# Pairing a convolution kernel's spectra by adding transfers in DRAM

## The chip, the cores and the metric

The kernel runs on one core of a Trainium2 chip. The metric is the device time of one execution in microseconds (us). The core has a matrix engine (PE), a vector engine (VectorE, DVE in the profile), an activation engine (ScalarE, ACT), GpSimd (POOL) and SyncE (SP). Each works through its own queue of instructions in order, and they wait for each other on semaphores. DMA transfers are issued by SP and GpSimd; in this kernel only GpSimd's transfers add to what lies at the destination.

## The reference

The program is two layers of the same pair: a long convolution over time (an S4 state-space layer) and a gated feed-forward net, each on a normalised input and with a residual. L = 2048 time steps, D = 512 channels, N = 128 states, F = 1376.

```python
dt = exp(log_dt);  A = A_re + 1j*A_im;  dB = dt * (B_re + 1j*B_im)
K = einsum("dn,dnl,dn->dl", C, exp((dt*A)[:, :, None] * l), dB).real   # one kernel of 2048 lags per channel
conv(u) = irfft(rfft(u, 2L) * rfft(K, 2L))[:L] + u * Dskip             # causal convolution and the direct term
x = x + conv(layernorm(x))
x = x + (silu(n @ w_gate) * (n @ w_up)) @ w_down                       # n = layernorm(x)
# ... and both lines once more with the same weights
```

The direct term `u * Dskip` is the same as adding `Dskip` to the kernel at lag 0. K depends on the parameters alone and is computed once, for both layers.

## The kernel before, in words

The program has two parts. The first, called the kernel stage here, computes K and its spectra and stores them in DRAM (array `wdr`) and in SBUF (`w0r`, for the first time block). The second runs the convolutions and the feed-forward nets block by block (512 time steps each) with products of spectra; it reads `wdr` from about 299 us on.

The kernel stage goes through the channels in eight chunks of 64 (DC, NCH). For one chunk:

- `gen_turns`, `gen_exp`, `gen_trig` (VectorE, ScalarE) make powers of the states; `gen_g` and `gen_e` (VectorE) make from them the two factors `g` and `re`/`im` of every lag. The last doubling step of `gen_g` is added by a GpSimd transfer from `acc` into `g` (L465).
- `lags` (PE, L485 and L486) multiplies the factors into `pk`: all 2048 lags of 64 channels.
- `spread_in` copies `pk` to `ks` (ScalarE, L491), and `spread` turns it round through DRAM (`kdr`) into `kt` (SP, L498 and L500); the last two chunks do it on PE instead (`spread_pe`).
- `spectra`, called for q0 = 0 and q0 = 1, multiplies `kt` with Fourier matrices on PE (`products`, L515) into the PSUM tile `pw`: two of four frequency classes q at a time, real and imaginary part i, NB = 4 blocks k of 512 lags. L517 adds the direct term as a product of a row of ones with `dsk`. What the convolution needs for block k is the sum of block k and of a signed, swapped copy of block k-1. ScalarE writes the signed copy of blocks 0 to 2 into `wo` (L542, twice) and block 0 into `w0r` (L543), VectorE adds blocks 1 to 3 from PSUM (L545), and SP stores the sum (`store_w`, L524): two transfers of 192 KB, in rows of 256 B.

Chunks 6 and 7 do part of this later by `first_parts` and `later_parts`, among the first convolution.

Beside the chunks run the sums of squares of the weights (`norms`): GpSimd loads a piece `st` (L317; three buffers under the tag w, which `scales` and the convolution use later), ScalarE squares it (L323), PE adds it over partitions into `nrm` (L326), and at the end of a group VectorE takes the maximum (L329). `second` computes input spectra `pf` (L289, L292, L293).

The order of all this is written out by hand. `at(t, f)` puts a step on a list with a time on a scale of about microseconds; `starts` holds each chunk's start, 28 or 31 apart; the list is sorted and run, and within `manual_schedule` the engines that it names issue in just this order. Before the change these are ScalarE, VectorE and PE, and SP in the chunk loop; GpSimd's order is found by the planner from its own estimates. `spectra` is a generator with four parts (products; ScalarE's copies; VectorE's addition; SP's stores), and `use` gives the time of each part. After the stage the planner orders every engine.

The tags name buffers: a tile waits until the last user of the tile before it under the same tag is done. `z` has one buffer, free in this stage; `sg` has one (for `wo` with q0 = 0), and with q0 = 1 `wo` is a piece of `spare`.

Of the kernel before, what the change touches and what calls it, by code (L numbers as in the profile page):

```python
# [11 lines left out]
F32 = mybir.dt.float32  # L12
# [10 lines left out]
P = 128  # L23
# [11 lines left out]
DC = 64  # L35
# [38 lines left out]
def kernel(ctx, tc, x, a_re, a_im, b_re, b_im, c_re, c_im, log_dt, d_skip,  # L74
# [62 lines left out]
    G.memset(ones, 1.0)  # L137
    onesb = sb.tile([P, P], BF16, name="onesb")
    G.memset(onesb, 1.0)
    one = sb.tile([P, 1], F32, name="one")  # L140
    G.memset(one, 1.0)
    hpi = sb.tile([P, 1], F32, name="hpi")
    G.memset(hpi, math.pi / 2)

# [333 lines left out]
    def lags(ts, g):  # L478
# [7 lines left out]
            PE.matmul(o, lhsT=g[:, 1, :, d], rhs=im[:, 0:64, d], start=False, stop=True, tile_position=(0, 32 * grp))  # L486
        return pk

    def spread_in(pk):
        ks = tl([P, 4, 16, 16], "ks", "nn")  # L490
        A.activation(ks, pk.rearrange("p d (c a) -> p a c d", a=4), AF.Copy)  # L491
        return ks
# [15 lines left out]
                          start=True, stop=True, tile_position=(0, 32 * ga))  # L508
        A.activation(kt, kp, AF.Copy)

    def products(ch, pw, kt, k0, k1, q, order):

        for i, c in order:
            e = ek[q // 2][:, q % 2, c - 1, i] if c else ef[:, q, i]
            PE.matmul(pw[:, i], lhsT=e, rhs=kt[:, :, c + 4 * k0:4 * k1:4, :].rearrange("p g k d -> p k g d"), start=c == 0, stop=c == 3)  # L515
            if (i, c) == (0, 0) and k0 == 0:
                PE.matmul(pw[:, 0, 0], lhsT=one[0:1].to_broadcast([1, P]), rhs=dsk[:, ch * DC:(ch + 1) * DC], start=False, stop=False)  # L517

    def signs(q):

        return enumerate((-1.0, 1.0) if q % 2 == 0 else (1.0, -1.0))

    def store_w(h, off, q, wo):
        nc.sync.dma_start(wdr[1:, h, q, :, :, off:off + DC].rearrange("k p i d -> p i k d"), wo.rearrange("p i k g d -> p i k (g d)"))  # L524

    def spectra(ch, kt, q0):


        h, off = ch // 4, (ch % 4) * DC
        pw = pbig([P, 2, 2, NB, 4, 16], "pw")  # L530
        for j in range(2):
            products(ch, pw[:, j], kt, 0, NB, q0 + 2 * j, [(i, c) for i in range(2) for c in range(4)])
        yield
        if q0:
            wo = spare[0][:, 16 * DC:].rearrange("p (j i k g d) -> p j i k g d", j=2, i=2, k=NB - 1, g=4)
        else:
            wo = tl([P, 2, 2, NB - 1, 4, 16], "wo", "sg")
        wf = pw.rearrange("p j i k g d -> p j i k (g d)")
        wv = wo.rearrange("p j i k g d -> p j i (k g d)")
        pv = pw.rearrange("p j i k g d -> p j i (k g d)")  # L540
        for i, sign in signs(q0):
            A.activation(wv[:, :, i], pv[:, :, 1 - i, :3 * DC], AF.Copy, scale=sign)  # L542
        A.activation(w0r[:, h, q0::2, :, off:off + DC], wf[:, :, :, 0], AF.Copy)  # L543
        yield
        V.tensor_tensor(wv, pv[:, :, :, DC:], wv, OP.add)  # L545
        yield
        for j in range(2):
            store_w(h, off, q0 + 2 * j, wo[:, j])
        yield

    def first_parts(c0, q):

        n, off = NCH - c0, (c0 % 4) * DC
        pw = pbig([P, 2, 8, 4, 16], "pw")[:, :, :n]
        for c in range(4):
            for i in range(2):
                e = ek[q // 2][:, q % 2, c - 1, i] if c else ef[:, q, i]
                PE.matmul(pw[:, i], lhsT=e, rhs=kt2[:, c0 + 2 - NCH:, :, c], start=c == 0, stop=c == 3)
                if (i, c) == (0, 0):
                    PE.matmul(pw[:, 0], lhsT=one[0:1].to_broadcast([1, P]), rhs=dsk[:, c0 * DC:], start=False, stop=False)  # L560
        A.activation(w0r[:, 1, q, :, off:], pw.rearrange("p i k g d -> p i (k g d)"), AF.Copy)

    def later_parts(ch, kt, qs=QORD):


        h, off = ch // 4, (ch % 4) * DC
        for q in qs:
            pw = psml([P, 2, NB - 1, 4, 16], "pw")
            products(ch, pw, kt, 1, NB, q, [(0, c) for c in range(4)])
            yield  # L570
            products(ch, pw, kt, 1, NB, q, [(1, c) for c in range(4)])
            yield
            w0 = w0r[:, h, q, :, off:off + DC].rearrange("p i (g d) -> p i g d", g=4)
            wo = next(slots)
            for i, sign in signs(q):
                A.activation(wo[:, i, 0], w0[:, 1 - i], AF.Copy, scale=sign)
                A.activation(wo[:, i, 1:], pw[:, 1 - i, :2], AF.Copy, scale=sign)
            V.tensor_tensor(wo, pw, wo, OP.add)
            store_w(h, off, q, wo)
            yield  # L580
# [344 lines left out]
                if m:  # L925
                    tops.append(m)

    with tc.manual_schedule(engines={mybir.EngineType.Activation, mybir.EngineType.DVE, mybir.EngineType.PE}):
        ts[0], ts[1] = gen_tiles(0), gen_tiles(1)
        ex = gen_exp(0, ts[0])  # L930

# [54 lines left out]
        def at(t, f, n=1):  # L986
            plan.append((t, len(plan), (lambda: take(f, n)) if hasattr(f, "__next__") else f))
# [17 lines left out]
        def factors(c, t):  # L1005

            at(t + 0.2, lambda: upper(ts[c]))

            def tiles():
                gs[c] = tl([P, 2, 32, DC], "g", ("ga", "gb")[c % 2])  # L1010
            at(t + 0.1, tiles)
            gg, ge = later(lambda: gen_g(c, ts[c], gs[c])), later(lambda: gen_e(ts[c]))
            for k in range(4):
                at(t + 0.2 + 2 * k, gg, 2)
            at(t + 0.3, ge)
            for k in range(5):
                at(t + 8.2 + k, gg)
            at(t + 22.0, ge, 100)

        def use(c, t):  # L1020

            box, kt, n = {}, kt2[:, c % 2], starts[c + 1]

            def copy():
                box["ks"] = spread_in(box["pk"])
                if c < NCH - 2:
                    spread(c, box["ks"], kt)
            at(t, lambda: box.update(pk=lags(ts[c], gs[c])))
            at(t + 7.1, copy)
            if c == NCH - 2:  # L1030
                at(t + 10.0, lambda: spread_pe(box["ks"], kt))
            at(t + 25.0, lambda: sizes(c, kt, box["ks"]))
            for q0, ats in list(enumerate(((t + 17.5, t + 25.2, n + 2.1, n + 9.0),
                                      (n + 6.9, n + 14.0, n + 17.3, n + 22.0))))[:2 if c < NCH - 2 else 1]:
                sp = later(lambda q0=q0: spectra(c, kt, q0))
                for t0 in ats:
                    at(t0, sp)
# [26 lines left out]
        for i in range(NCH - 1):  # L1064
# [3 lines left out]
            second_block(i, t)  # L1068
            if i + 2 < NCH:
                prepare(i + 2, t)  # L1070
            for k, t0, t1, t2, t3 in ((0, -1.4, 8.0, 13.9, 17.0), (1, 8.1, 14.5, 17.45, 19.5),
                                      (2, 15.0, 26.5, 28.05, 36.0)):
                n = ((3, 3, 0), (3, 3, 0), (3, 3, 0), (3, 2, 0), (3, 2, 0), (3, 3, 0), (3, 3, 3))[i][k]
                if i == NCH - 2 and k == 2:
                    t0, t1, t2, t3 = 15.0, 20.0, 24.0, 27.0
                if n:
                    weights(n, t + t0, t + t1, t + t2, t + t3)
# [53 lines left out]
        norm = first_norm(tl([P, 2, D], "nn1", "hf"))  # L1131
        take(conv[0], 1)
        spread_pe(ks, kts[1])
        take(conv[0], 1)
        scales()
        split(1, 0)
# [99 lines left out]
```

## Time and profile before

| | us |
|---|---|
| median of three executions | 1191.86 |
| lowest and highest | 1186.78, 1192.82 |
| the profiled execution | 1186.51 |
| its span in the profile | 1184.7 |
| PE, VectorE, ScalarE, GpSimd busy | 1117.3, 1006.2, 587.1, 92.2 |
| lag products of chunk 0 and chunk 7 end (ks copy starts) | 69.18, 274.26 |

In the rows of the profile, L515 is a line of the kernel, then come the engine and the operation, written tile <- read tiles, sizes as partitions x elements, and a count. In a timeline the first two numbers are the start and the length in us of a run of equal instructions, and square brackets hold how long the engine had been idle before and what it waited for. An fp32 matmul appears as two rows. A row of POOL with DMA_DIRECT2D is the time in which GpSimd makes a transfer, not the transfer itself; in the list of DMA issues the last number is the median time from issue to landing. In the view by source line the three numbers behind the count are minimum, median and maximum in ns. In the stretch view each engine has its busy time and its number of instructions, then come the granted clock, the share of the DMA engines and GB/s.

### The profile page before, as it was taken

The page shows a single profiled execution, that of the slowest core. Times are in us where ns is not written, and L with a number is a line of the kernel's source. Part 1 is how long each engine was busy: PE and PEld are TensorE (multiplying, and loading weights), DVE is VectorE, ACT ScalarE, POOL GpSimd, SP SyncE. Part 2 cuts the span into 40 slices and gives each one's busy share as a digit, 9 for nine tenths or more (in the row PEclk, how much of TensorE's full clock was granted, in tenths as well). Part 3 has the DMA queues.
Part 4 walks back from the last instruction along what each step waited for, and adds up shares of the span by engine and source line. Part 5 has one row for each costly group of instructions (what it writes and reads, how often), then busy time and mean ns, then how long its engine had stood idle before and what let it go on. Part 6 is the DMA issues. An engine that isn't in the chain of part 4 may idle for free.

```text
span 1184.7 us, 24523 instructions
## 1 busy us (share of the span) xinstructions
PE 1117.3 (94%) x10008; PEld 884.8 (75%) x10008; DVE 1006.2 (85%) x1591; ACT 587.1 (50%) x1180; POOL 92.2 (8%) x151
## 2 busy tenths in 40 slices
PE   1979999999789988999999999989999999999998
PEld 1868888888776857777778687858777686876875
DVE  7999999987789898999899999989994899983211
ACT  6677888833461554546654443655533452324211
POOL 1011111110000010002000000211000010000000
PEclk9989999999899999999999999999999999999999
DMA  6266666757484337432353354333544144312000
GB/s 231 91 162 149 162 166 162 182 179 240 125 271 140 115 119 200 118 96 84 92 152 128 112 165 155 96 104 115 149 116 165 46 121 130 118 49 45 14 24 18
DMA packets 136532, 151.17 MB, mean 128 GB/s; under 512 B 75474, under 2 KB 83666, under 8 KB 136419
## 3 DMA queue, kind: packets, MB, share of 16 engines
q1 hardware_dynamic: 129314, 126.47, 35.8%
q0 software_dynamic: 7104, 23.14, 7.3%
q8 instruction: 78, 1.28, 0.5%
q14 instruction: 36, 0.29, 0.1%
HBM read 101.85 MB, written 31.46 MB: 113 GB/s over the span
## 4 chain that ended last, share of the span: by engine, by line
PE 37%; DVE 27%; issue 4%; DMA 4%; ACT 2%; SPq 1%; POOL 0%; DVEq 0%; ACTq 0%; POOLq 0%
PE pgu L886 6%; PE pgu L887 6%; PE pgu L889 6%; DVE t L754 5%; DVE yk L757 5%; PE py L901 4%; PE py L902 3%; PE py L903 3%; PE pi L773 3%; PE pf L273 3%; DVE yk L754 2%; DVE z L229 2%; DVE sg L893 2%; DMA mix<-nn 1%; DVE bb L229 1%
## 5 line engine op out<-in xcount | busy, mean ns | idle before, releaser
L886 PE MATMUL pgu<-mix,wsl 128*128 128x256 f16 x1280 | 299.7, 273 | 6.9 <-DVE sg L893 4.4
L887 PE MATMUL pgu<-mix,wsl 128*128 128x256 f16 x1280 | 299.7, 273 | 0.0
L889 PE MATMUL pgu<-mix,wsl 128*128 128x256 f16 x1280 | 195.6, 273 | 0.0
L887 PEld LDWEIGHTS <-wsl 128*128 128x128 f16 x1280 | 125.5, 98 | 24.3 <-issue 8.0
L901 PE MATMUL py<-wsl,hh 128*128 128x512 f16 (+1 forms) x352 | 134.2, 381 | 8.6 <-DVE xg L906 6.9
L886 PEld LDWEIGHTS <-wsl 128*128 128x128 f16 x1280 | 125.4, 98 | 16.0
L889 PEld LDWEIGHTS <-wsl 128*128 128x128 f16 x1280 | 125.5, 98 | 14.9
L903 PE MATMUL py<-wsl,hl 128*128 128x512 f16 (+1 forms) x352 | 134.1, 381 | 0.2 <-DVE hl L895 0.2
L902 PE MATMUL py<-wsl,hh 128*128 128x512 f16 x320 | 121.8, 381 | 0.0
L754 DVE TENSOR_TENSOR t<-uu,w 128x1024 f32<-128x1024 f32 x96 | 116.9, 1218 | 2.6 <-DMA w<-wdr 2.4
L757 DVE TENSOR_TENSOR yk<-yk,t 128x1024 f32<-128x1024 f32 x96 | 116.9, 1217 | 0.3
L892 ACT ACTIVATE sg<-pgu,sc 128x512 f32<-128x512 f32 x80 | 54.6, 683 | 121.0 <-PE pgu L889 115.9
L893 DVE SCALAR_TENSOR_TENSOR sg<-pgu,sc,sg 128x512 f32<-128x512 f32 x80 | 59.6, 745 | 56.6 <-ACT sg L892 56.5
L515 PE MATMUL pw<-kt,ek 128*128 128x256 f32 (+1 forms) x384 | 94.1, 382 | 0.0
L894 ACT ACTIVATE hh<-sg 128x512 f16<-128x512 f32 x80 | 50.0, 626 | 76.1 <-DVE sg L893 76.0
L773 PE MATMUL pi<-yl,mix 128*128 128x256 f16 x576 | 78.9, 273 | 5.0 <-DVE yl L229 2.7
L515 PEld LDWEIGHTS pw<-kt,ek 128*128 128x128 f32 x384 | 70.8, 194 | 8.9
L273 PE MATMUL pf<-z,eh 128*128 128x256 f16 x576 | 74.9, 273 | 0.0
L754 DVE TENSOR_TENSOR yk<-u,w0r 128x1024 f32<-128x1024 f32 x56 | 68.2, 1218 | 1.5 <-ACT u L275 1.5
L902 PEld LDWEIGHTS <-hh 128*128 128x128 f16 (+1 forms) x352 | 34.6, 98 | 46.1 <-issue 10.6
L895 DVE TENSOR_TENSOR hl<-sg,hh 128x512 f16<-128x512 f32 x80 | 54.8, 686 | 15.6 <-ACT hh L894 15.5
L485 PE MATMUL pk<-re,g 128*32 128x64 f32 x1024 | 65.0, 317 | 2.8 <-DVE re L440 2.8
(239 smaller groups left out, 2154.3 us busy)
## 6 DMA issues: line engine op xcount, KB each, us to landing
w<-wdr SPq DMA_DIRECT2D x96, 256.0 KB, 2.7
uu<-udr SPq DMA_DIRECT2D x96, 256.0 KB, 3.0
udr<-u POOLq DMA_DIRECT2D x32, 256.0 KB, 2.7
g<-acc POOLq DMA_DIRECT2D x6, 1024.0 KB, 8.4
udr<-u SPq DMA_DIRECT2D x16, 256.0 KB, 2.1
n<-ndr SPq DMA_DIRECT2D x16, 256.0 KB, 3.9
n<-xdr SPq DMA_DIRECT2D x4, 1024.0 KB, 5.7
kdr<-ks SPq DMA_DIRECT2D x6, 512.0 KB, 2.7
```

Source lines behind the costliest of these rows:

```text
L273: PE.matmul(pf[:, o], lhsT=e, rhs=m, start=k == 0, stop=k == len(terms) - 1)
L515: PE.matmul(pw[:, i], lhsT=e, rhs=kt[:, :, c + 4 * k0:4 * k1:4, :].rearrange("p g k d -> p k g d"), start=c == 0, stop=c == 3)
L754: V.tensor_tensor(t, uu.unsqueeze(1).to_broadcast([P, 2, 2, HD]), w.unsqueeze(2).to_broadcast([P, 2, 2, HD]), OP.mult)
L757: V.tensor_tensor(yk, yk, t, OP.add)
L773: PE.matmul(pi[:, o], lhsT=e, rhs=m, start=k == 0, stop=k == len(terms) - 1)
L886: PE.matmul(o, lhsT=wgu(wi, k, 0)[:, fs], rhs=nh[:, k], start=k == 0, stop=False)
L887: PE.matmul(o, lhsT=wgu(wi, k, 1)[:, fs], rhs=nh[:, k], start=False, stop=False)
L889: PE.matmul(o, lhsT=wgu(wi, k, 0)[:, fs], rhs=nlo[:, k], start=False, stop=k == 3)
L893: V.scalar_tensor_tensor(sg, pgu[:, 1], sc6[:, 4:5], sg, OP.mult, OP.mult)
L901: PE.matmul(py[:, r], lhsT=hh[:n, f, rc], rhs=wd(f, 0)[:n], start=f == 0, stop=False)
L902: PE.matmul(py[:, r], lhsT=hh[:n, f, rc], rhs=wd(f, 1)[:n], start=False, stop=False)
L903: PE.matmul(py[:, r], lhsT=hl[:n, f, rc], rhs=wd(f, 0)[:n], start=False, stop=f == FT - 1)
```

## The change

Three things change, all in the kernel stage.

1. The direct term leaves the products: L517 and L560 (the same in `first_parts`) go, and a new step `skip` adds `dsk` to lag 0 of `kt` on VectorE, on the first partition.
2. The sum of the two copies is made in DRAM. ScalarE copies blocks 1 to 3 from PSUM into a new tile `wa` (tag z), SP stores the signed copy `wo`, and GpSimd then issues the same two transfers from `wa` with an addition. VectorE's L545 goes. The parts of `spectra` are now products; ScalarE's copies; SP's stores; GpSimd's adding transfers.
3. GpSimd is named in `manual_schedule`, so its instructions go out in source order. Some times change with it: the last part of `spectra`, the maxima of the weights' sums, and the four last steps of `gen_e`, which are now separate entries.

```diff
+    def skip(ch, kt):
+
+        k = kt[0:1, :, 0]
+        V.tensor_tensor(k, k, dsk[:, ch * DC:(ch + 1) * DC].rearrange("p (g d) -> p g d", g=4), OP.add)
...
-    def products(ch, pw, kt, k0, k1, q, order):
+    def products(pw, kt, k0, k1, q, order):
...
-            if (i, c) == (0, 0) and k0 == 0:
-                PE.matmul(pw[:, 0, 0], lhsT=one[0:1].to_broadcast([1, P]), rhs=dsk[:, ch * DC:(ch + 1) * DC], start=False, stop=False)
...
-    def store_w(h, off, q, wo):
-        nc.sync.dma_start(wdr[1:, h, q, :, :, off:off + DC].rearrange("k p i d -> p i k d"), wo.rearrange("p i k g d -> p i k (g d)"))
+    def store_w(h, off, q, wo, eng=nc.sync, **add):
+        eng.dma_start(wdr[1:, h, q, :, :, off:off + DC].rearrange("k p i d -> p i k d"), wo.rearrange("p i k g d -> p i k (g d)"), **add)
...
+        wa = tl([P, 2, 2, NB - 1, 4, 16], "wa", "z")
...
             A.activation(wv[:, :, i], pv[:, :, 1 - i, :3 * DC], AF.Copy, scale=sign)
+        A.activation(wa.rearrange("p j i k g d -> p j i (k g d)"), pv[:, :, :, DC:], AF.Copy)
         A.activation(w0r[:, h, q0::2, :, off:off + DC], wf[:, :, :, 0], AF.Copy)
-        yield
-        V.tensor_tensor(wv, pv[:, :, :, DC:], wv, OP.add)
         yield
         for j in range(2):
             store_w(h, off, q0 + 2 * j, wo[:, j])
+        yield
+        for j in range(2):
+            store_w(h, off, q0 + 2 * j, wa[:, j], G, accum_op=OP.add)
         yield
...
-                if (i, c) == (0, 0):
-                    PE.matmul(pw[:, 0], lhsT=one[0:1].to_broadcast([1, P]), rhs=dsk[:, c0 * DC:], start=False, stop=False)
...
-    with tc.manual_schedule(engines={mybir.EngineType.Activation, mybir.EngineType.DVE, mybir.EngineType.PE}):
+    with tc.manual_schedule(engines={mybir.EngineType.Activation, mybir.EngineType.DVE, mybir.EngineType.PE, mybir.EngineType.Pool}):
...
-            at(t + 22.0, ge, 100)
+            for k in range(4):
+                at(t + 22.0 + 0.6 * k, ge, 1 if k < 3 else 100)
...
+            at(t + (17.1 if c < NCH - 2 else 12.5), lambda: skip(c, kt))
...
-            for q0, ats in list(enumerate(((t + 17.5, t + 25.2, n + 2.1, n + 9.0),
-                                      (n + 6.9, n + 14.0, n + 17.3, n + 22.0))))[:2 if c < NCH - 2 else 1]:
+            for q0, ats in list(enumerate(((t + 17.5, t + 25.2, n + 2.1, n + 7.5),
+                                      (n + 6.9, n + 14.0, n + 17.3, n + 21.0))))[:2 if c < NCH - 2 else 1]:
...
-            for k, t0, t1, t2, t3 in ((0, -1.4, 8.0, 13.9, 17.0), (1, 8.1, 14.5, 17.45, 19.5),
+            for k, t0, t1, t2, t3 in ((0, -1.4, 8.0, 13.9, 22.3), (1, 8.1, 14.5, 17.45, 22.9),
...
         spread_pe(ks, kts[1])
+        skip(c, kts[1])
```

In `weights(n, t0, t1, t2, t3)` the four times are those of a group's loads, squares, products and maximum.

More of the change, by code (lines that the diff above doesn't have):

```diff
@@ L531, in spectra @@
         for j in range(2):
-            products(ch, pw[:, j], kt, 0, NB, q0 + 2 * j, [(i, c) for i in range(2) for c in range(4)])
+            products(pw[:, j], kt, 0, NB, q0 + 2 * j, [(i, c) for i in range(2) for c in range(4)])
         yield
@@ L568, in later_parts @@
             pw = psml([P, 2, NB - 1, 4, 16], "pw")
[L569 removed]
+            products(pw, kt, 1, NB, q, [(0, c) for c in range(4)])
             yield
[L571 removed]
+            products(pw, kt, 1, NB, q, [(1, c) for c in range(4)])
             yield
```

2 lines of the change are left out of this document (removed).

## The prediction

> **What bounds the kernel now.** I read the page first, then the stretch view, then the timelines of PE, ScalarE, VectorE and GpSimd over one round of the kernel stage, and last the groups and DMA issues of what the change touches. The stage handles eight chunks of 64 channels, and a round runs from the end of one chunk's lag products (L485, L486) to the next.
>
> ```profile
> span 1184.7 us, 24523 instructions
> PE 1117.3 (94%) x10008; PEld 884.8 (75%) x10008; DVE 1006.2 (85%) x1591; ACT 587.1 (50%) x1180; POOL 92.2 (8%) x151
> ...
> 98.20:242.90 144.70, 144.70 (x1750) 122.91 (x1750) 139.00 (x164) 118.44 (x264) 22.76 (x43) 1.00 0.68 170
> ```
>
> In the 144.7 us of five rounds PE has no gap (columns PE, PEld, DVE, ACT, POOL), at full clock. VectorE is idle for only 5.7 us, ScalarE for 26.3. PE paces the stage and VectorE is close behind, so the page's 50% for ScalarE says nothing about this stage.
>
> ```profile
> 127.45 0.70 PE L515 MATMUL pw<-kt,ef 128*128 128x256 f32 x2
> ...
> 139.46 0.60 PE L326 MATMUL nrm<-sq,onesb 128*128 128x344 bf16 x3
> 139.90 0.59 PE L515 MATMUL pw<-kt,ef 128*128 128x256 f32 x2
> 140.43 0.43 PE L517 MATMUL pw<-tdk,one 1*128 1x64 f32 x2
> ...
> 142.18 0.59 PE L515 MATMUL pw<-kt,ef 128*128 128x256 f32 x2
> ...
> 143.91 0.59 PE L515 MATMUL pw<-kt,ef 128*128 128x256 f32 x2
> ...
> 148.01 0.49 PE L485 MATMUL pk<-re,g 128*32 128x64 f32 x8
> ...
> 156.37 0.70 PE L515 MATMUL pw<-kt,ef 128*128 128x256 f32 x2
> ```
>
> This round is 127.45 to 156.37 = 28.9 us; below, E is its start (127.45) and times are after E. PE does one spectrum (q0=1 of the chunk before), squares' sums (nrm) and pf, at E+12.0 the second nrm group, then spectrum q0=0, and at E+20.6 the lag products, 8.4 us.
>
> ```profile
> 127.64 1.02 ACT L491 ACTIVATE ks<-pk 128x1024 f32<-128x1024 f32 x1 [4.78 <-PE pk L486]
> 128.56 1.24 ACT L323 ACTIVATE sq<-st 128x344 bf16<-128x344 f32 x3
> ...
> 135.77 0.87 ACT L542 ACTIVATE spare<-pw 128x384 f32<-128x384 f32 x2
> 136.53 0.39 ACT L543 ACTIVATE w0r<-pw 128x256 f32<-128x256 f32 x1
> 136.79 1.26 ACT L323 ACTIVATE sq<-st 128x344 bf16<-128x344 f32 x3
> 138.07 1.28 ACT L395 ACT_TABLE_LOAD   x1
> ...
> 148.29 0.93 ACT L542 ACTIVATE wo<-pw 128x384 f32<-128x384 f32 x2
> ```
>
> ScalarE is idle once a round, 4.8 us before ks. It ends the second group of squares at 138.05, 1.4 us before PE needs it (139.46).
>
> **The change part by part.** *Direct term out of the products.* Eight products without it take 143.91-142.18 = 1.73 us, with it 142.18-139.90 = 2.28. Each of the two-pass L517 rows thus costs 0.55 us, 2.2 us in a round of four. PE alone would need 28.9-2.2 = 26.7.
>
> *Direct term into lag 0 (skip).* One VectorE addition of 64 elements on one partition. L454 (64 elements on 128 partitions, 0.22, row below) is nearest; I take 0.25 us. It waits for the kt loads, and behind it wait L435 and all later E-steps on VectorE, and PE's products. In the steady round it stands where the second L545 stood, at E+10.5, with the last kt load issued about 1.5 into the row below and landed 3.6 later, E+9.1, and PE there at E+11.5; in the first round VectorE comes later than PE:
>
> ```profile
> 78.71 2.74 DVE L386 CUSTOM_DVE_ANT_0 im<-im 128x256 uint16<-128x256 uint16 x4
> 81.37 2.29 DVE L435 TENSOR_TENSOR re<-re 128x2048 f32<-128x2048 f32 x1
> ...
> 79.42 0.67 PE L515 MATMUL pw<-kt,ef 128*128 128x256 f32 x2 [1.06 <-DMA kt<-kdr]
> ...
> 131.39 2.04 SPq L500 DMA_DIRECT2D kt<-kdr  x4
> ```
>
> There skip stands behind the doubling L386 until 81.4, so the products start 2.3 us later; less two L517 this round loses 1.2.
>
> *L545 off VectorE.*
>
> ```profile
> 121.95 0.95 DVE L545 TENSOR_TENSOR wo<-pw,wo 128x768 f32<-128x768 f32 x1
> 122.82 0.22 DVE L454 TENSOR_TENSOR g<-g,spare 128x64 f32<-128x64 f32 x1
> ...
> 138.86 0.95 DVE L545 TENSOR_TENSOR spare<-pw,spare 128x768 f32<-128x768 f32 x1
> 139.73 2.28 DVE L435 TENSOR_TENSOR re<-re 128x2048 f32<-128x2048 f32 x1
> ```
>
> By their starts 0.87 us each, 1.74 a round, less 0.25 for skip: VectorE's busy time falls from 139.0/5 = 27.8 to 26.3 a round, below PE's. The moved maxima (L329) and the split of the four E-steps change no amount of work; they put the maxima where their sums exist.
>
> *A third copy (wa) on ScalarE.* 768 elements out of PSUM lie between the 384 of L542 (0.87/2) and the 1024 of L491 (0.92 by starts): 0.75 us, 1.5 a round, inside the 4.8 idle. But the one at E+9.1 stands before the second squares, whose end moves from E+10.6 to E+11.35, while PE, two L517 shorter, now wants it at E+10.9. So PE waits 0.4; from there 0.15 for the last nrm, 8.1-1.1 for the spectrum and 8.4 for the lags make a round of 26.95. Every further us X that ScalarE stands still before those squares lengthens the round by X: the gain is 2.0-X, and the 1.4 us of cover at this place is what hid it before.
>
> *Where X comes from: the adding transfers.* wa has one buffer. Its copy at E+9.1 waits until both adding transfers of the spectrum before have landed. These run on GpSimd's queue, 384 KB in two, each of 768 pieces of 256 B.
>
> ```profile
> L465 POOL DMA_DIRECT2D g<-acc x6: 1237/1272/1294, 78.4 to 225.6; - x6
> L317 POOL DMA_DIRECT2D st<-in_B_w_gate_dram x16: 536/556/584, 101.3 to 187.0; - x16
> L706 POOL DMA_DIRECT2D udr<-u x32: 539/542/607, 410.9 to 886.4; - x32
> ...
> g<-acc POOLq DMA_DIRECT2D x6, 1024.0 KB, 8.4
> ...
> kt<-kdr SPq DMA_DIRECT2D x24, 128.0 KB, 3.6
> ...
> xg<-in_A_u_dram SPq DMA_DIRECT2D x3, 1024.0 KB, 5.7
> ...
> st<-in_B_w_gate_dram POOLq DMA_DIRECT2D x16, 172.0 KB, 3.4
> ...
> wdr<-wo SPq DMA_DIRECT2D x14, 192.0 KB, 3.4
> ```
>
> GpSimd's time G for one: L317 (172 KB) and L706 (256 KB) have 128 pieces and the same 0.54 to 0.56, so pieces count and not bytes; the only adding one, L465, has 256 and 1.27, that is 5.0 ns a piece. For 768 that is 3.8 us. The ends are 0.55 (a price per transfer) and 0.54+640*5.7 ns = 4.2 (the slope from 128 to 256). I take 3.8, from the row that also adds. R, from the end of G to landing: 3.4-0.6 = 2.8 as the plain store of the same pieces from SP, up to 8.4-1.3 = 7.1 as L465; the 1 MB addition lands 1.5 times as late as a 1 MB load (8.4 against 5.7), so I take 3.5.
>
> [...]
>
> The clock of the chain: the signed copies of q0=0 (148.29, E+20.8) move 0.75 later with the wa before them and end at E+22.5, 4.5 before the next E. SP stores at once (these stores moved ahead of kdr and kt in SP's queue, which is empty there), the first lands 3.4 later, and GpSimd starts at E-1.0. Landed: E-1.0+2G+R = E+10.1, wanted E+9.1, so X = 1.0. Behind the wait stand w0r, the second squares, and through PE's nrm the spectrum and the lags. Behind the pair on GpSimd stand, in source order now, the three loads for the second squares (0.55 each; the last is issued at E+7.7 and lands 3.4 later at E+11.1, wanted at E+10.95+X: covered), then the memsets and L465, which lands at E+8.3+8.4 = E+16.7, 1.8 before the lags need it. The other adding pair starts at E+12.6 and lands at E+23.7; wa wants its buffer at E+22.6, and the 1.1 fits into what is left of ScalarE's idle time. The loads for the next round's first squares follow at E+20.2 and land at E+24.7, 3 before they are wanted. GpSimd's round is 4*3.8 + 6*0.55 + 1.3 = 20 of 28 us. The new bytes could also hold up the kt loads (3.6); PE has 1 us of slack there, I add nothing and leave it to the range.
>
> **Sum.**
>
> ```profile
> 69.18 1.02 ACT L491 ACTIVATE ks<-pk 128x1024 f32<-128x1024 f32 x1 [5.20 <-PE pk L486]
> 98.40 1.02 ACT L491 ACTIVATE ks<-pk 128x1024 f32<-128x1024 f32 x1 [5.68 <-PE pk L486]
> ...
> 242.89 1.02 ACT L491 ACTIVATE ks<-pk 128x1024 f32<-128x1024 f32 x1 [4.94 <-PE pk L486]
> ...
> 274.26 1.03 ACT L491 ACTIVATE ks<-pk 128x1024 f32<-128x1024 f32 x1 [7.69 <-PE pk L486]
> ...
> 279.92 0.43 PE L560 MATMUL pw<-tdk,one 1*128 1x64 f32 x2
> 280.28 0.43 PE L558 MATMUL pw<-kt,ef 128*128 128x64 f32 x2
> ```
>
> First round (to 98.40): +1.2. Five rounds (to 242.89): -5*(2.0-1.0) = -5.0. Last round (to 274.26), where ScalarE has no exponentials and wa's buffer is free in time: four L517, 2.2, less 0.3 that PE waits for the squares behind wa, -1.9. Then four L560 at about 0.45 by their starts, 1.8, half of it on PE's path: -0.9. Together -6.6 us; later stages have the same work and shift. The profiled execution took 1186.51 us (its span plus 1.8), which would become 1179.9; the median of the runs is 1191.86, 0.45% above it, and against that I forecast **1185**.
>
> **Rivals.**
> - *The addition lands late.* R is that of L465, 7.1: ScalarE's wait for wa takes the place of the work saved, X = 7.6+7.1-10.1 = 4.6, sum +1.2+5*2.6-1.9-0.9 = +11.4, 1203. It decides from 2G+R = 12.4 (X 2.3) on. [...] Against: 192 KB is a fifth of L465's bytes. Within X = 2.3 to 3.5 it is still under 0.5%.
> - *Generation or landing is cheap.* X = 0, sum +1.2-10-1.9-0.9 = -11.6: 1180. For it: L317's flat 0.55.
> - *Nothing arrives.* The stage ends earlier, but the later stages, ordered by the planner and fed by the weight loads, give it back: 1192. Against: those loads start when the same engines free their buffers.
> [...]
>
> **How the numbers follow.** Chances: forecast (X 0.3 to 2) 0.40, cheap 0.24, late 0.22, nothing 0.12, starved 0.02. The forecast's own range is 1180 to 1190; it is over 0.5% faster up to X = 1.1, about three fifths of it. 0.5% (6 us) is about what a measurement of this kernel can tell from no change. Faster 0.24+0.26 = 0.50; slower: the late and starved cases beyond X = 3.5 and some disturbance of the planner's order, 0.28; same 0.22. Range 1174 (cheap, with the runs' lower level of 1186.8) to 1201 (late, nearly whole).
>
> **What would show it.** No row with tdk and one; L515 groups of 1.73 throughout; no L545; POOL rows for wdr of about 3.8 us; ScalarE's wa with a wait on a DMA of 1 us at E+9; ks rows 28 us apart. Wrong if those POOL rows are under 2 or over 5 us, if ScalarE waits over 2.3 us at wa, if the second squares or skip wait for loads, or if the ks of 274.26 comes 7 us earlier and the end does not.

## The result and the profile after

The changed kernel takes 1203.87 us (median of 20 executions, 1188.23 to 1211.50); the kernel before, beside it, 1186.91 us (median of 20, 1183.12 to 1192.82). The ratio is 1.0107, 95% interval 1.0082 to 1.0132: slower by about 1%. The ratio is one of means and leaves out the five executions of the changed kernel that are more than 1.5% above its fastest; the medians, which contain them, stand at 1.0143. The profiled execution took 1204.58 us, with a span of 1202.8 against 1184.7. The lines have moved: L518 are the products (L515 before), L483 and L484 the lag products, L494 the copy to `ks`, L501 and L503 the way through `kdr` to `kt`, L490 is `skip`, L545 the copy to `wa`, L525 the stores and the adding transfers, L463 the 1 MB addition into `g`.

From the page:

```profile
span 1202.8 us, 24436 instructions
PE 1110.1 (92%) x9948; PEld 882.1 (73%) x9948; DVE 996.9 (83%) x1586; ACT 594.9 (49%) x1193; POOL 133.0 (11%) x176
```

The stretch view, for 98.20 to 242.90 as in the prediction, for the stage up to 270 and for a piece of one round:

```profile
98.20:242.90 144.70, 126.97 (x1439) 108.92 (x1431) 118.56 (x140) 116.64 (x264) 49.27 (x57) 0.93 0.92 178
98.20:270.00 171.80, 154.07 (x1795) 131.92 (x1787) 141.12 (x166) 128.59 (x279) 59.28 (x67) 0.93 0.91 180
145.85:152.30 6.45, 6.45 (x17) 5.21 (x18) 3.71 (x6) 6.36 (x5) 5.01 (x5) 0.55 0.88 78
```

ScalarE's timeline, the copies to `ks` that end each chunk's lag products:

```profile
69.30 1.02 ACT L494 ACTIVATE ks<-pk 128x1024 f32<-128x1024 f32 x1 [5.13 <-PE pk L484]
98.78 1.02 ACT L494 ACTIVATE ks<-pk 128x1024 f32<-128x1024 f32 x1 [3.65 <-PE pk L484]
131.30 1.02 ACT L494 ACTIVATE ks<-pk 128x1024 f32<-128x1024 f32 x1 [4.34 <-PE pk L484]
163.45 1.02 ACT L494 ACTIVATE ks<-pk 128x1024 f32<-128x1024 f32 x1 [3.87 <-PE pk L484]
...
288.21 1.02 ACT L494 ACTIVATE ks<-pk 128x1024 f32<-128x1024 f32 x1 [2.69 <-PE pk L484]
```

PE and VectorE have less work, as forecast (7.2 and 9.3 us less busy), and both now stand still in the stage: where PE was busy for all of 144.70 us it is busy for 126.97, at a mean granted clock of 0.93 instead of 1.00, and the DMA engines' busy share has gone from 0.68 to 0.92. The five rounds from 98.78 on are 31.0 to 33.8 us long instead of some 29. From the first `ks` to the last it is 218.91 us against 205.08 before (69.18 to 274.26): 13.8 of the 18.1 us are lost there.

Who waits for `kt` in the stage (view of waits, 98.2 to 270; total, times, longest):

```profile
DVE kt L490 <- DMA kt<-kdr: 15.7, 4, 6.5
...
PE pw L518 <- DMA kt<-kdr: 13.7, 4, 4.1
```

The list of DMA issues:

```profile
g<-acc POOLq DMA_DIRECT2D x6, 1024.0 KB, 9.1
wdr<-wa POOLq DMA_DIRECT2D x26, 192.0 KB, 5.4
...
kdr<-ks SPq DMA_DIRECT2D x6, 512.0 KB, 4.2
kt<-kdr SPq DMA_DIRECT2D x24, 128.0 KB, 7.1
```

`kt` lands 7.1 us after its issue; it was 3.6. ScalarE's copy to `wa`, where the prediction put its wait, is not among the waits there. One round of the changed kernel in the timelines of GpSimd, SP and PE:

```profile
127.88 3.31 POOL L525 DMA_DIRECT2D wdr<-wa  x2 [7.95 <-DMA wdr<-wo]
...
135.06 1.25 POOL L463 DMA_DIRECT2D g<-acc  x1 [0.19 <-issue]
...
135.69 2.61 SPq L503 DMA_DIRECT2D kt<-kdr  x4
...
145.85 1.19 PE L518 MATMUL pw<-kt,ef 128*128 128x256 f32 x2 [3.12 <-DMA kt<-kdr]
146.83 2.77 PE L518 MATMUL pw<-kt,ek 128*128 128x256 f32 x6
149.39 1.06 PE L518 MATMUL pw<-kt,ef 128*128 128x256 f32 x2
150.24 2.15 PE L518 MATMUL pw<-kt,ek 128*128 128x256 f32 x6
152.22 0.59 PE L518 MATMUL pw<-kt,ef 128*128 128x256 f32 x2
```

The round starts at 131.30. Two adding transfers of the spectrum were issued just ahead of it and landed by 134.3; the 1 MB addition into `g` goes out at 135.06 and lands 9.7 us later, and the `kt` loads go out from 135.69 on, just behind it. PE idles 3.12 us for `kt`, and then pays again: its first four groups of `L518` rows take 152.22-145.85 = 6.4 us, where the next four take 3.46 (two times 1.73), and the granted clock of that piece is 0.55. Wait and slow restart cost 3.1+2.9 = 6.0 us here. This is one of the two rounds with the longest slow stretch: the granted clock is 0.50 for 6.83 us in these two and for 3.41 us in the other three. From 98.2 to 270 PE idles 171.80-154.07 = 17.7 us, and it is busy at half clock for 20.9 us, which costs half of that, some 10.

The remaining 4 us come at the end of the stage. VectorE's row of the last chunk's `skip` and PE's first row of `first_parts`, from the timelines of the changed kernel:

```profile
292.99 0.21 DVE L490 TENSOR_TENSOR kt<-kt,tdk 1x64 f32<-1x64 f32 x1 [9.60 <-ACT kt L512]
...
298.33 0.59 PE L562 MATMUL pw<-kt,ef 128*128 128x64 f32 x4
```

VectorE stands 9.6 us for ScalarE's copy of `kt`, with a product of the convolution and the scales of the weights behind it. `first_parts` starts 298.33-288.21 = 10.1 us after the last `ks`; before, it was 279.66-274.26 = 5.4.

### The profile page after: what moved, and what is told of

Its sections match the earlier page's. It is cut to its first block, busy times and chain, and to the rows that moved or that the text cites. A ratio compares the mean times of both kernels' runs of the same rounds, so it can differ in the third digit from the quotient of the medians.

```text
span 1202.8 us, 24436 instructions
## 1 busy us (share of the span) xinstructions
PE 1110.1 (92%) x9948; PEld 882.1 (73%) x9948; DVE 996.9 (83%) x1586; ACT 594.9 (49%) x1193; POOL 133.0 (11%) x176
## 3 DMA queue, kind: packets, MB, share of 16 engines
q0 software_dynamic: 27488, 28.25, 12.6%
## 4 chain that ended last, share of the span: by engine, by line
PE 33%; DVE 27%; issue 5%; DMA 4%; ACT 2%; SPq 1%; POOL 1%; DVEq 0%; POOLq 0%; ACTq 0%
PE pgu L888 6%; PE pgu L889 6%; PE pgu L891 6%; DVE t L756 5%; DVE yk L759 4%; PE py L903 3%; PE py L904 3%; PE py L905 3%; DMA mix<-nn 3%; DVE yk L756 2%; PE pi L775 2%; PE pf L271 2%; DVE z L227 2%; DVE hl L897 1%; DVE sg L895 1%
## 5 line engine op out<-in xcount | busy, mean ns | idle before, releaser
L518 PE MATMUL pw<-kt,ek 128*128 128x256 f32 (+1 forms) x384 | 99.2, 399 | 0.0
L518 PEld LDWEIGHTS pw<-kt,ek 128*128 128x128 f32 x384 | 79.0, 210 | 11.1
L775 PEld LDWEIGHTS <-mix 128*128 128x128 f16 x576 | 56.1, 98 | 14.1 <-issue 3.4
```

The costliest lines, as they stand in the source:

```text
L775: PE.matmul(pi[:, o], lhsT=e, rhs=m, start=k == 0, stop=k == len(terms) - 1)
```

## The experiments

Two theories of `kt`'s lateness. A: the 1 MB addition into `g` comes out some 4 us after a round's start (3.4 to 4.9, in the first round 6.1; before mostly 11 to 12: 139.17 in the round from 127.64) and meets the `kt` loads. B: the adding transfers of the spectra themselves hold up what shares the DMA engines with them. The column "stage" is the time from the first `ks` to the last in the one profiled execution, "kt" the median landing, the ratio is against the kernel before on the same chip.

| run | edit | stage | kt | ratio, 95% interval |
|---|---|---|---|---|
| before | | 205.1 | 3.6 | 1 |
| after | | 218.9 | 7.1 | 1.0107 (1.0082, 1.0132) |
| e1_noadd | no adding transfers | 194.3 | 4.0 | 0.9907 (0.9877, 0.9937) |
| e2_glate | addition into g later | 210.7 | 4.1 | 1.0067 (1.0041, 1.0094) |
| e3_skiplate | last skip behind the scales | 220.7 | 7.7 | 1.0046 (1.0023, 1.0070) |
| e4_direct | direct term alone | 199.4 | 3.5 | 0.9926 (0.9902, 0.9949) |
| e5_plain | e3, plain stores for the adds | 201.1 | 5.1 | 0.9901 (0.9869, 0.9934) |
| e6_gdve | e3, no 1 MB addition | 208.0 | 3.2 | 1.0025 (1.0005, 1.0045) |
| e7_half1 | e3, adds for q0=1 only | 197.2 | 3.7 | 0.9932 (0.9910, 0.9954) |
| e8_planner | e3, GpSimd's order planned | 212.0 | 3.9 | 1.0028 (1.0009, 1.0046) |
| e9_half0 | e3, adds for q0=0 only | 219.1 | 5.6 | 1.0100 (1.0074, 1.0127) |
| e10_fill | e3, 14 more products | 221.5 | 7.6 | 1.0095 (1.0060, 1.0130) |
| e11_wide | e3, adds in rows of 1536 B, elsewhere | 196.1 | 3.4 | 0.9866 (0.9839, 0.9893) |
| e12_rows | e3, array in rows of 1536 B | 194.0 | 3.2 | 0.9946 (0.9916, 0.9977) |
| e13_fill7 | e3, 7 more products | 211.7 | 5.3 | 1.0037 (1.0021, 1.0053) |

**Without the adding transfers.**

```diff
-        for j in range(2):
-            store_w(h, off, q0 + 2 * j, wa[:, j], G, accum_op=OP.add)
```

> Leaves out the adding transfers from wa (L525 of the changed kernel): what is stored is the signed copy alone, so the spectra lack blocks 1 to 3; all else, the copies into wa too, is as in the changed kernel. Theory B (the adding transfers' own packets, 256 B read, added and written in DRAM, are what holds up kdr and kt): kt lands about 4 us after its issue as before, PE's waits for kt go, the rounds of the kernel stage fall from 31-32.5 to 27-28 us and the program is 12 to 15 us shorter than the changed kernel, 5 under the one before. Theory A (the 1 MB addition g<-acc, now issued about 4 us after a round's start and together with the kt loads, holds them up): kt still lands after 6.5 to 7 us, rounds stay at 30 to 32, and the time changes by less than 4 us against the changed kernel.

Theory B's numbers came: `kt` 4.0, no wait of PE for it, the granted clock 1.00, and the stage 24.6 us shorter than in the changed kernel; by the ratios the program gained as much, more than the 12 to 15 us expected. The stage is also 10.8 shorter than in the kernel before, with all the other edits in place. Theory A is not excluded, because the 1 MB addition moved too: VectorE, no longer ahead of a late PE, releases it mostly 8 to 9 us after a round's start (162.54 in the round from 154.44), behind the `kt` loads. The early addition is thus partly a consequence of the late PE.

**The addition into g later.**

```diff
+                yield
                 G.dma_start(g[:, :, 16:32].rearrange("p i b d -> p i (b d)"), ..., accum_op=OP.add)
...
+            at(starts[c] - 13.3, gg, 2)
...
+                if k == 0 and i:
+                    t0 = -13.4
```

> The changed kernel with the 1 MB addition g<-acc issued some 11 us after a round's start instead of 4 (behind the loads of the next round's first squares, which are moved ahead of it); the adding transfers of the spectra stay. Theory A: the kt loads land about 4 us after issue, PE's waits for kt and the half-clock stretches behind them go, rounds are 27 to 28.5 us, and the program ends 12 to 18 us before the changed kernel, 1186 to 1192. Theory B: kt lands after 6.5 to 7 us as in the changed kernel, rounds stay at 31 to 32, time within 4 us of the changed kernel's 1204.

Half of A: `kt` lands after 4.1 and PE no longer waits for it, but the rounds are still about 30 us. The view of waits of this kernel says where the time went, and its list of DMA issues why:

```profile
PE pk L484 <- DMA g<-acc: 15.5, 5, 3.4
DVE g L449 <- DMA g<-acc: 15.4, 4, 5.3
```

```profile
g<-acc POOLq DMA_DIRECT2D x6, 1024.0 KB, 9.4
wdr<-wa POOLq DMA_DIRECT2D x26, 192.0 KB, 9.4
```

The addition now shares the engines with the other pair of adding transfers, both land 9.4 us after issue, and the lag products wait for `g` instead (PE, five waits of up to 3.4 us). By the ratios the program gained 0.4%, some 5 us of the 12 to 18 expected. Moving one transfer moved the wait.

**The last skip behind the scales.**

```diff
         spread_pe(ks, kts[1])
-        skip(c, kts[1])
         take(conv[0], 1)
         scales()
+        skip(c, kts[1])
```

> The changed kernel with the last chunk's skip moved behind the scales on VectorE, so that VectorE no longer stands 9.6 us for ScalarE's copy of kt with the scales and two products of the convolution behind it. Theory: the rounds of the kernel stage stay as they are (last ks at 288), what follows the last ks comes 4 to 5 us earlier, time 1199 to 1200. Rival: the waits come back at the next place that needs kt (first_parts on PE) or at the loads of the weights: under 1.5 us gained.

The first theory holds: `first_parts` starts at 293.41, 5.4 us after the last `ks` (288.00) instead of 10.1, and the ratio falls by 0.6%, some 7 us instead of the 4 to 5 expected; 4.7 are these, and where the rest comes from isn't shown. In the traces at hand the time from the last `ks` to the end of the span is 913.5 to 917.9 us in the three kernels with the early skip, 904.4 to 914.6 in the others, 910.4 before.

**The direct term alone.**

```diff
-                PE.matmul(pw[:, 0, 0], lhsT=one[0:1].to_broadcast([1, P]), rhs=dsk[:, ch * DC:(ch + 1) * DC], start=False, stop=False)
...
+            at(t + (17.1 if c < NCH - 2 else 12.5), lambda: skip(c, kt))
...
         scales()
+        skip(c, kts[1])
```

> The kernel before with part 1 of the change alone: no products with a row of ones, lag 0 of kt gets the direct term on VectorE, at the times of the changed kernel; sums stay on VectorE, no adding transfers of spectra, GpSimd's order from the planner, the maxima and the steps of gen_e where they were; the last chunk's skip stands as in the changed kernel. If VectorE and PE are as close as the profile before says, PE saves 2.2 us a round but VectorE, 27.8 us of a round and 0.25 more, becomes the bound: rounds 28.0 to 28.4 instead of 28.9, 3 to 5 us from the stage, of which the wait at the last skip takes about 4: 1183 to 1189. If skip in front of VectorE's chain waits for kt (landing 3.6 us after issue, needed as the second addition was), the rounds stay at 28.9 or grow: 1189 to 1196.

The expectation misdescribes one point: the last skip stood behind the scales in this kernel, so the wait of 4 us is not in it. The stage is 5.7 us shorter and the program 0.74% faster. VectorE is busy for 165.6 of the 171.8 us from 98.2 to 270 and PE for 163.3: VectorE is the busier of the two. Part 1 is good by itself with the last skip in this place; what it cost in the changed kernel is the wait at the last chunk. The loss in the rounds came with the rest of the change, and e1_noadd, which keeps part 3, puts it on the adding transfers of part 2.

**Plain stores in place of the adds.**

```diff
-            store_w(h, off, q0 + 2 * j, wa[:, j], G, accum_op=OP.add)
+            store_w(h, off, q0 + 2 * j, wa[:, j], G)
```

> As the run with the last skip moved (e3_skiplate), but GpSimd's transfers from wa store plainly and add nothing: the same pieces to the same addresses at the same places of the queue, so the spectra lose the signed copy. Theory B1 (the addition itself is dear: an adding packet of 256 B took 46 ns in the changed kernel, a plain one 18): kt lands after about 4 us, PE's waits for kt go, rounds are 27 to 28.5 and the time 14 to 20 us under e3_skiplate's 1195. Theory B2 (any further 768 pieces of 256 B in front of kdr and kt do it): kt still 6 us or more, rounds 30 or more, within 6 us of e3_skiplate.

B1: the same bytes to the same rows, without the addition, cost little, and the time is the one expected. `kt` lands at 5.1, between the two theories, and PE does not wait for it; the addition into `g` goes out 1.1 to 4.2 us behind the first `kt` load in every round. One round of 33.1 us stands out (208.28 to 241.35), in which PE waits for squares of weights whose loads were late; the others take 26.0 to 29.4. The pages show what the addition changes. The rows are the GpSimd queue's packets, megabytes and share of 16 engines' span; first of the changed kernel, then of e5_plain, of e12_rows (below) and of the kernel before:

```profile
q0 software_dynamic: 27488, 28.25, 12.6%
```

```profile
q0 software_dynamic: 8768, 28.25, 9.3%
```

```profile
q0 software_dynamic: 10848, 28.25, 10.3%
```

```profile
q0 software_dynamic: 7104, 23.14, 7.3%
```

The kernel before lacks these 26 transfers. A plain one adds (8768-7104)/26 = 64 packets, an adding one (27488-7104)/26 = 784, one for each piece of 256 B and 16 of 4 B. In time of all 16 engines an adding transfer takes (12.6% of 1202.8 - 7.3% of 1184.7)/26 = 2.5 us and a plain one (9.3% of 1174.9 - 86.5)/26 = 0.9; lengthened packets of other transfers on this queue are contained in both.

**No 1 MB addition into g.**

```diff
-            if n == 16 and 0 < ch < NCH - 1:
+            if False:
```

> As e3_skiplate, but the last doubling step of g is added by VectorE, as in the other steps (one product and two additions of 1024 elements more, 2.5 us a round net), and no 1 MB transfer adds. Adding transfers of the spectra stay. If the 1 MB addition beside them is what kt needs to be late: kt about 4 to 5 us, PE waits little, VectorE sets the rounds at 28.5 to 29.5, time 1183 to 1190. If the adding transfers of the spectra alone hold kt up: kt stays at 6.5 to 7.5, rounds 31 to 33, 1194 to 1200.

`kt` lands after 3.2 us although the adding transfers of the spectra are all there, which points to the 1 MB addition (A). VectorE, with the doubling back, is busy for 95% of the stretch, and the rounds are 29.7 us on average, so little is won.

The landing times of the single transfers in the traces say the same. In the changed kernel both adding transfers of the spectrum have landed 0.4 to 3.0 us before the first `kt` load goes out, in all five rounds. Of the 18 loads whose landing is recorded, the four that go out within 0.8 us of the start of GpSimd's row for `g` land after 2.7 to 4.9 us, the 14 later ones after 6.5 to 8.5. In all fifteen traces together, chunk 0 left out, the 53 loads that went out more than 0.9 us behind that start and before the addition had landed took 6.5 to 11.5 us, the 187 with no such addition in flight 2.6 to 7.2, with a median of 3.5, and the 27 in between 2.6 to 8.3. So the 1 MB addition is what `kt` meets.

What the spectra's transfers do (B) is to change the order. Here are the first of the five rounds in the changed kernel (`ks` at 98.78) and in e1_noadd (99.29); their four `kt` loads landed after 2.7, 3.0, 7.1 and 7.6 us and after 4.0 to 4.6:

```profile
104.86 1.26 POOL L463 DMA_DIRECT2D g<-acc  x1 [2.36 <-DVE acc L462]
105.04 1.75 SPq L503 DMA_DIRECT2D kt<-kdr  x4
```

```profile
104.14 1.95 SPq L503 DMA_DIRECT2D kt<-kdr  x4
105.45 1.26 POOL L463 DMA_DIRECT2D g<-acc  x1 [2.57 <-DVE acc L462]
```

The addition comes 6.1 and 6.2 us after `ks`, at the same place. But the store to `kdr`, issued while the adding transfers of the spectrum were in flight, lands after 5.2 us instead of 3.8, so the `kt` loads fall behind the addition. From then on PE is late, the addition comes earlier still, and the order stays so. Adding transfers of spectra can also hold up `kt` themselves where they are still in flight: in e6_gdve's round from 127.30 the loads took 4.2 to 7.2 us. No run sends the addition ahead of `kt` without adds of the spectra before it, so it is not shown that it would be late then too.

**Half of the adds.** In e7_half1 only q0=1 is paired by adding transfers, in e9_half0 only q0=0; the other spectrum is summed on VectorE as before.

```diff
+        dram = q0 == 1        # e9_half0: q0 == 0
...
+        if not dram:
+            V.tensor_tensor(wv, pv[:, :, :, DC:], wv, OP.add)
```

> As e3_skiplate, but the spectrum q0=0 is summed on VectorE and stored by SP as in the kernel before; only q0=1 is paired by adding transfers. The adds that end at a round's start, just ahead of kdr and kt, are gone; those in the middle of a round stay. If it is those at the round's start that set kt back: kt about 4 us, rounds 27.5 to 28.5, time 1176 to 1184. If the total of the added traffic counts, wherever it stands: about half of the loss stays, rounds 29 to 30, 1185 to 1190.

> The other half of e7_half1: q0=0 is paired by adding transfers, issued just ahead of a round's start; q0=1 is summed on VectorE and stored by SP. If the place decides (adds beside kdr, kt and the 1 MB addition of g): kt 6 us or more, PE waits for it, rounds 30 to 31.5, 1186 to 1194. If the amount decides: as e7_half1, kt about 4 us, rounds 27.5 to 28.5, 1176 to 1184.

The place decides. The adds in the middle of a round (12 transfers in all) cost `kt` nothing that shows: `kt` 3.7, stage 197.2, and `kdr` lands after 2.7 us, as before. Those ahead of a round's start (14) bring the whole loss back: `kdr` lands after 4.1 us, the addition goes out ahead of `kt` in three of the five rounds, PE waits three times for `kt`, up to 4.9 us, and twice for VectorE, which stands in `skip` up to 8.2 us for `kt`; the stage is 219.1.

**GpSimd's order from the planner.**

```diff
-    with tc.manual_schedule(engines={..., mybir.EngineType.PE, mybir.EngineType.Pool}):
+    with tc.manual_schedule(engines={..., mybir.EngineType.PE}):
```

> As e3_skiplate, but GpSimd's order is the planner's again, as in the kernel before: the adding transfers, the 1 MB addition of g and the loads of the squares interleave otherwise. If the source order of GpSimd is what lets the 1 MB addition out at the time of the kt loads: kt 4 to 5 us, 5 to 10 us under e3_skiplate. If the traffic itself sets it, whatever the order: within 4 us of e3_skiplate's 1195, with PE's waits at kt or at g.

Mixed: `kt` is back at 3.9 and the stage 8.7 us shorter than in e3_skiplate, but 6.9 longer than before, with new waits (its view of waits, 98.2 to 270):

```profile
ACT wa L545 <- DMA wdr<-wa: 21.6, 5, 8.5
...
DVE g L449 <- DMA g<-acc: 11.7, 3, 5.4
```

By the ratios the program gained 0.2%, and the two intervals overlap. As in e2_glate, another order chooses another victim; here it is ScalarE at `wa`, the wait that the prediction had feared.

**Long rows.** First the same adds to an unused part of the array in rows of 1536 B, then the whole array laid out so.

```diff
-    wdr = dram.tile([NB, 2, 4, P, 2, HD], F32, name="wdr")
+    wdr = dram.tile([2, 4, P, 4, 2, NB - 1, DC], F32, name="wdr")
...
+        eng.dma_start(wdr[h, q, :, off // DC].rearrange("p i k d -> p (i k d)"), wo.rearrange("p i k g d -> p (i k g d)"), **add)
...
+                    for i in range(2):
+                        nc.sync.dma_start(w[:, i].rearrange("p (c d) -> p c d", c=4), wdr[h, q, :, :, i, k - 1])
```

> As e3_skiplate, but the adding transfers add the same 192 KB each to an unused part of the array in rows of 1536 B instead of 256 (that part is first filled by eight further stores at the start; the spectra lose the second copy, and the adds no longer wait for SP's stores). If the price of an addition is one per piece (46 ns for 256 B, so 20 thousand of them): the GpSimd queue has a sixth of the packets and about half of the added time, kt lands at about 4 us, rounds 27.5 to 29, 1176 to 1186. If it is one per byte: the packets are longer in proportion, kt 6 us or more, rounds 30 to 32, 1190 to 1197.

> As e3_skiplate, with the array of spectra laid out so that every transfer of a pair of copies, the plain one and the adding one, writes rows of 1536 B (128 pieces for 192 KB instead of 768); its readers in the convolution take each 256 KB as two loads of 512 pieces of 256 B. All of the computation is done. If the price of the addition is one per piece: kt about 4 us, rounds 27.5 to 28 as in e11_wide, last ks at 262 to 267; the readers' loads, 2.7 us to landing before, land at 3 to 5 us and are hidden: 1170 to 1178. If the shorter rows of the readers are not hidden, VectorE waits for w in the convolutions and the program is at 1180 or more though the last ks comes as early.

The diff is that of e12_rows. The price goes largely by pieces: a transfer takes (10848-7104)/26 = 144 packets, and a packet of 1536 B takes 140 ns where one of 256 B takes 46 (medians in the traces), so the queue's added time (10.3% above) falls to half, not to a sixth. With `kt` at 3.2, e12_rows has all the additions and a stage of 194.0 us: as short as with none, 11.1 under before. The store to `kdr` still lands after 4.2 us (4.3 in the first round), but the addition into `g` goes out 1.5 to 4.8 us behind the first `kt` load in every round; how much of the gain is this order isn't separated from the price. The median, 1180.18, is a gain of 0.5%, less than the 11 us of the stage and in the range of the second theory, though VectorE's waits for `w`, now read in pieces of 256 B, are only 6.5 us in all, against 3.8 in the changed kernel. The profiled execution, whose stage this is, took 1175.95, 4 us less than the median, and its span keeps 1184.7-1174.2 = 10.5 of the 11.1 us; the ten executions spread from 1171 to 1189. Why they do isn't settled.

**Products in PE's gap.** Products of constants, overwritten by the real ones, ahead of the q0=0 spectrum of chunks 1 to 5: 14 in e10_fill, 7 in e13_fill7.

```diff
+        if q0 == 0 and 0 < ch < NCH - 2:
+            for _ in range(14):
+                PE.matmul(pw[:, 0, 0]..., lhsT=ef[:, 0, 0], rhs=ef[:, 0, :2]..., start=True, stop=True)
```

> As e3_skiplate, with 14 further products (about 3 us of PE work that needs nothing but loaded constants, written over by the real ones) in front of the q0=0 spectrum of chunks 1 to 5, where PE waits for kt. If PE's gap costs twice, once as the wait and again as the stretch at half the granted clock behind it (16 products in 6.4 us instead of 3.5), then PE, busy through the wait, keeps its clock: 2 to 3 us less a round in spite of 3 us more work, last ks at 275 to 280 instead of 288, 1183 to 1188. If the clock is not tied to the gap: rounds as in e3_skiplate or up to 3 us longer where PE does not wait, last ks 288 to 296, 1195 to 1203.

> As e10_fill with 7 further products instead of 14, 3 us of PE work (14 took 6.1 us, as much as the wait and the stretch at half clock together). If the gap costs twice: PE keeps its clock, the products run 3.46 us for 8 instead of 6.4, and the rounds are about 3 us shorter than in e3_skiplate and e10_fill: 28 to 30, last ks at 274 to 280, 1182 to 1189. If the half clock is not tied to the gap: rounds as in e3_skiplate, last ks 286 to 290, 1193 to 1198.

The 14 took 6.1 us and not 3 (each is two rows, 0.43 us in all), so the time, which came out in the range of the second theory, does not tell the two apart: e10_fill puts 5*6.1 = 30.5 us of work in the place of about as much loss. In e3_skiplate PE idles 171.80-151.85 = 20.0 us and is busy at half clock for 18.8, which costs 9.4; together 29.4. In e10_fill it hardly idles and keeps its clock, and the stage is only 0.8 us longer with all that work in it. So the loss is more than the waits: half again as much. With 7 the rounds shorten. The stretch 98.20 to 270.00 of e3_skiplate, of e10_fill and of e13_fill7, and one filler:

```profile
98.20:270.00 171.80, 151.85 (x1776) 130.04 (x1775) 139.43 (x165) 128.00 (x279) 58.54 (x66) 0.94 0.91 179
```

```profile
98.20:270.00 171.80, 171.67 (x1933) 150.22 (x1927) 140.71 (x165) 127.67 (x277) 59.67 (x67) 1.00 0.89 176
```

```profile
98.20:270.00 171.80, 166.86 (x1882) 144.48 (x1882) 147.16 (x170) 132.13 (x287) 63.60 (x71) 0.99 0.92 187
...
140.59 3.18 PE L534 MATMUL pw<-ef 128*128 128x256 f32 x14
```

Adding 3.2 us of work to each of five rounds shortened the stage by 9.0 us (220.7 to 211.7). That a gap in these rounds costs its wait and the slow restart behind it is shown (20.0 and 9.4 us in e3_skiplate); that all of the 9.0 is clock isn't, since `kt` also landed earlier (5.3 against 7.7). The program shows little of it: 1.0037 against 1.0046, with a time between the two that were expected.

## Why the prediction was wrong

The forecast was 1185 and faster; it came out slower, at 1203.87, above the range's upper end of 1201.

- *The step that failed* is "The new bytes could also hold up the kt loads (3.6); PE has 1 us of slack there, I add nothing and leave it to the range." The loads landed 3.5 us later (7.1), and from 98.2 to 270 PE lost 17.7 us to gaps and some 10 to half clock. What held them up is the 1 MB addition into `g` going out ahead of them, which the new transfers bring about by holding up `kdr`; without the one (e6_gdve), with it at another place (e2_glate) or without adds ahead of the round's start (e1_noadd, e7_half1) `kt` lands after 3.2 to 4.1 us. The step weighed bytes; the same bytes cost little as plain stores (e5_plain, `kt` 5.1 us, stage 201.1) and in long rows (e12_rows, 3.2 and 194.0).
- *L463's place was wrong*, and with it the order that the step relied on. It was put at E+8.3, behind `kt`; in the round shown it went out at E+3.8 (135.06 after 131.30). The pair ahead of it on GpSimd was issued by 131.2 already, and GpSimd then waits for VectorE alone (5.1 us in four waits in the stage), which hardly waits for PE and so runs ahead of a late one; this last is argued, not isolated by a run. In e1_noadd, where PE is not late, it goes out at E+8.1 to E+9.0 from the second of the five rounds on.
- *The work saved was sized right in sum, partly by luck.* With X = 0 the terms up to the last `ks` are +1.2-10.0-1.9 = -10.7; e1_noadd, without the adds, gave -10.8 and e12_rows, with them, -11.1. But the terms were not these: first round, five rounds and last round gave +0.2, -7.7 and -3.2 in e1_noadd and -0.5, -7.4 and -3.2 in e12_rows. The sizes of the single steps hold (the prediction's eight products are eight rows, that is four products; the price stands): four groups of L518 rows take 3.46 us at full clock, `skip` 0.21, the `wa` copy 0.84 (0.75 in the sum).
- *G and X were mis-sized.* G was put at 3.8 and measured 1.65 (below), under the 2 us that the prediction named as a sign of being wrong; the pieces count, but at 1652/768, about 2 ns each, and not 5. With a landing 5.4 us after issue the buffer was free in time: ScalarE waited at `wa` once in the whole stage, 2.1 us, in the last round.

```profile
L525 POOL DMA_DIRECT2D wdr<-wa x26: 1587/1652/2312, 95.6 to 288.1; - x26
```

GpSimd's time for one transfer is not flat: 1.65 us for 768 adding pieces, 1.00 for the same plain (e5_plain), 0.94 for 128 adding ones of 1536 B (e12_rows; medians).

- *The last chunk's skip was not costed.* The prediction costed the steady and the first round's skip, not the last, which stands ahead of `scales` in VectorE's queue. That is the 9.6 us wait and 4.7 us of the path.
- *The rival of 1203* had the right number by luck, with the wrong mechanism: it put a wait of 4.6 us a round on ScalarE at `wa`. In e8_planner that wait does appear, five times and up to 8.5 us.
- *The starved case*, 0.02 of the chances: no run shows what it rests on. GpSimd's 26 rows of L525 took 1.59 to 2.31 us, all under the forecast's 3.8.
- "The stage ends earlier, but the later stages give it back" is not borne out where the stage did get shorter: in e1_noadd it is 10.8 us shorter and the whole 0.93% (11 us), and in e12_rows' profiled execution 10.5 of 11.1 us reach the end. Only the median of e12_rows keeps less, 0.5%.

Three kernels that do all of the computation beat both: the direct term alone (0.9926), with q0=1 paired besides (0.9932), and the long rows (0.9946); their intervals overlap.

## What to carry to other kernels

Cost an adding transfer by its pieces and by what shares the DMA engines with it at that moment, not by its bytes alone: here 192 KB went out as 784 packets and took 2.5 us of all 16 engines in rows of 256 B, 144 packets and 1.3 us in rows of 1536 B (e12_rows), and the adds in the middle of a round left `kt` at 3.7 us (e7_half1) where those ahead of its start left it at 5.6 (e9_half0). Lay the destination out in long rows, or keep it away from small transfers on the path of the bounding engine. Look at the order in which transfers leave different queues: a small delay of one (here of `kdr`, 5.2 us to landing instead of 3.8 in the round from 98.78) can put the loads behind it behind a large transfer, and then costs more than the delay (`kt` at 7.1 us instead of 3.6). Where such an engine has to wait, add what it pays for the restart (here 2.9 us behind a wait of 3.1). And look at every place where a moved step stands in its engine's queue, the last iteration above all.

## What was not expected of the hardware

- A GpSimd transfer with an addition went out as one packet for each piece of 256 B (784 a transfer), the same transfer without it as 64 packets: 2.5 against 0.9 us of all 16 engines by the queue's share.
- Behind a 1 MB addition in flight, loads of 128 KB took 6.5 to 11.5 us (53 loads of five kernels); with none in flight 187 such loads took 2.6 to 7.2, with a median of 3.5. Two that went out within 0.6 us of the start of GpSimd's row for it were not late: 2.7 and 3.0 us in the changed kernel (105.04).
- With each of PE's five gaps in the stage of the changed kernel, 3.1 to 4.1 us long, the granted clock fell to 0.50 for 3.41 or 6.83 us, beginning 2.1 to 4.3 us after the gap's start. In the same run a gap of 2.99 us (291.87 to 294.85) was followed by 3.41 us at 0.50 from 294.99 on; one of 3.32 us before the first `ks` (57.57 to 60.89) was not, and the clock stayed at 1.00.
